# One copy of the folded weights per row group, token-major first sums, reciprocals on GpSimd, filler matmuls at the start

## The chip, the cores and the metric

The kernel runs on one core of one Trainium2 chip. The metric is the device time of one execution in microseconds (us), median of several runs. Engines are named as the profile names them: PE is TensorE (PEld its weight loads), ACT ScalarE, DVE VectorE, POOL GpSimd, SP SyncE, whose queue (SPq) issues 381 of the 400 DMA instructions in the trace of the kernel before. Each engine is given its own list of instructions.

## The reference, cut

Two stages of attention between 4 x 12416 tokens of 128 channels and 32 inducing points, then a gated feed-forward layer with 1536 hidden channels.

```python
def mab(q, kv):
    s = scale * (q @ kv.transpose(0, 2, 1))
    s = s - s.max(-1, keepdims=True)
    a = np.exp(s)
    a /= a.sum(-1, keepdims=True) + 1e-09
    return a @ kv
h = mab(I, x)                      # 32 rows per batch: sums over all tokens
attn = mab(x, h)                   # every token looks at the 32 rows
gate = 1.0 / (1.0 + np.exp(-(attn @ w_gate)))
return (gate * (attn @ w_val)) @ w_out
```

## The kernel before: the parts that matter

The second attention is never multiplied out. `h` is folded into the gate and value weights once per batch (`fold`), so a token needs only its 32 attention weights. The tokens are processed in units of 512 (25 units per batch, the last one a short tail of 128). A unit has six `G` steps (two gate matmuls, row-packed, into one of two PSUM buffers), six `T` steps (a 128x1024 tanh on ScalarE), twelve `V` steps (one value matmul into one of three PSUM buffers), twelve products (`D` on VectorE, or `C` on ScalarE with `P` on GpSimd), twelve `W` steps (four output matmuls each) and one evacuation of the accumulator `ACC` by ScalarE (`E`). Every engine's list is written out in a table `ORDER`, so the order was chosen ahead of time.

The fold, three times 1024 columns per batch, with `hT` (`h` transposed) repeated four times so that all four row groups of the array get both weights:

```python
hT = [sb(f"hT{q}", [P, 4, M]) for q in range(2)]
hw = [sb(f"hw{q}", [P, 2 * F]) for q in range(2)]
def fold(b, j, eng):
    def em(o):
        t = psl(o)
        for k, w in ((0, wg), (1, wv)):
            PE.matmul(t[:, k * TOK : (k + 1) * TOK], lhsT=hT[q][:].rearrange("c a m -> c (a m)"), rhs=w[:, j * TOK : (j + 1) * TOK],
                      start=True, stop=True)
    # ... one copy of 1024 columns to hw, on ACT (on DVE for j == 1 of batch 0)
```

The rows of a later quad (16 tiles of 128 tokens): score, exponential, a DMA transpose, a tree of sums on GpSimd, the reciprocal on VectorE, the multiplication on GpSimd, then more DMA:

```python
def tree(o):                                                     # on GpSimd
    # ... pairwise sums of 32 into TREE
    POOL.tensor_tensor(out=sm_b.t[:, 0:ng], in0=TREE[:, 0:ng, 0], in1=TREE[:, 0:ng, 1], op=ALU.add)
rc = dve(160, [tr] + rc_b.old, f"rc{b}.{i}", lambda o: DVE.reciprocal(out=rc_b.t[:, 0:ng], in_=sm_b.t[:, 0:ng]))
# ... mult(o) on GpSimd: n_b = t_b * rc_b, then bt (DMA transpose), wr, re (DMA)
```

Batch 0 does without DMA transposes in its first sums: x is transposed by TensorE, scores come out with the inducing points on the partitions, and TensorE transposes them back (`ap`) before the sums over tokens (`hp`). The three weights are cast by ScalarE (`wg`, `wv`, `wo`). Which products go to GpSimd: `COPIES = (3,)`, one of twelve in every unit. GpSimd's list begins with the casts of x and then, at once, the loads of batch 1 (`... cx5.8 cx5.0 ld1.0 ld1.1 tr0.1 mu0.1`).

The softmax here doesn't subtract the row's maximum and nothing guards it: scores larger than these inputs give would overflow.

## Time and profile before

| | |
|---|---|
| median of 3 runs | 714.0 us (712.83 to 714.18) |
| first tanh of the units | 31.65 us into the trace |
| eleventh evacuation of `ACC` | 122.3 us |
| end of the trace | 712.5 us |

The page of the kernel before: busy time of each engine with its share of the span, and the span in 40 slices of 17.8 us (a digit is the busy share in tenths; PEclk is the clock granted to TensorE).

```profile
PE 679.3 (95%) x7928; PEld 382.2 (54%) x7928; DVE 677.4 (95%) x1156; ACT 685.2 (96%) x884; POOL 336.5 (47%) x449
...
PE   5799999999999999999999999999999999999998
...
ACT  3989999999999999999999999999999999999994
POOL 6354446355354374364462642643634535526431
PEclk9959999999999999999999999999999999999999
```

Three engines are at 95%, and one slice near the start has half the clock. The view by windows of the kernel before (window, its length, busy us and instructions of each engine, granted clock, DMA share, GB/s):

```profile
0.00:31.65 31.65, 21.16 (x337) 14.69 (x338) 13.91 (x34) 18.81 (x30) 15.70 (x30) 1.00 0.95 318
31.65:34.50 2.85, 1.16 (x7) 0.28 (x5) 1.50 (x3) 2.85 (x5) 1.89 (x5) 1.00 0.25 49
34.50:51.60 17.10, 16.68 (x137) 7.63 (x136) 12.31 (x21) 14.49 (x18) 8.83 (x13) 0.50 0.60 96
51.60:122.30 70.70, 68.50 (x811) 37.89 (x808) 68.31 (x117) 70.56 (x95) 34.76 (x48) 1.00 0.79 148
122.30:702.00 579.70, 564.70 (x6555) 316.63 (x6552) 574.51 (x974) 576.99 (x739) 275.02 (x354) 1.00 0.40 96
```

The five busy figures are PE, PEld, DVE, ACT, POOL. From 34.5 to 51.6 us, at half clock, ScalarE is busy 14.49 of 17.10 us and VectorE 12.31. Afterwards both are nearly always busy. (At the very start the clock record has no entry yet; the first matmuls are slower all the same: a 512-wide score matmul takes 0.61 us at 12.4 us and 0.39 us at 18.1 us.)

The view of groups by form of the kernel before (count, then busy us in all, mean ns of one, and idle time before):

```profile
L625 DVE SCALAR_TENSOR_TENSOR ua<-tga,v 128x512 f16<-128x512 f16 x1056 | 648.7, 680 | 13.7 <-PE v L625 3.7 <-ACT tga L625 3.4 <-PE g L625 2.4
L625 ACT ACTIVATE tga<-g 128x1024 f16<-128x1024 f32 x576 | 562.0, 1078 | 3.5 <-PE v L625 1.0 <-PE g L625 0.5 <-ACT e L625 0.3
...
L625 ACT COPY vs<-v 128x512 f32<-128x512 f32 x96 | 60.9, 634 | 1.6 <-PE v L625 1.2
...
L625 ACT CAST hw<-g 128x1024 f16<-128x1024 f32 x11 | 11.6, 1059 | 0.1
...
L625 DVE RECIPROCAL rc<-sm 128x16 f32<-128x16 f32 x19 | 4.6, 244 | 0.0
```

A mean here is the span of one instruction, and neighbours overlap. The distance from start to start, where an engine has work queued, is what an instruction costs its engine: 0.904 us for the tanh, 0.466 for a 512-wide copy, 0.598 for a product on VectorE, 0.163 for a row reciprocal.

### The profile page before, as it was taken

To read this page: it belongs to the slowest core of one execution; us is meant where nothing else is said; L and a number is where in the kernel's file an instruction comes from. 1 tells how busy PE (TensorE), PEld (TensorE's weight loads), DVE (VectorE), ACT (ScalarE), POOL (GpSimd) and SP (SyncE) were. 2 spreads that over 40 slices of the span, in tenths; PEclk is the share of its full clock that TensorE was granted. 3 is DMA by queue.
4 is the path that set the end of the run, shared out by engine and by line. 5 is a ranking of instruction groups with operands and counts; after the bars stand their busy time and mean duration, and the time that the engine had idled before them with its cause. 6 is when DMAs were issued, how large, how long until landed. Compare 5 with 4: busy or idle time off the path is not lost.

```text
span 712.5 us, 20005 instructions
## 1 busy us (share of the span) xinstructions
PE 679.3 (95%) x7928; PEld 382.2 (54%) x7928; DVE 677.4 (95%) x1156; ACT 685.2 (96%) x884; POOL 336.5 (47%) x449
## 2 busy tenths in 40 slices
PE   5799999999999999999999999999999999999998
PEld 3445555555565555555555555555555555555555
DVE  2679999999999999999999999999999999999997
ACT  3989999999999999999999999999999999999994
POOL 6354446355354374364462642643634535526431
PEclk9959999999999999999999999999999999999999
DMA  9868769475445753456435464223221222131111
GB/s 360 213 111 149 129 133 187 113 133 102 111 115 99 168 112 70 117 131 132 106 97 102 94 148 98 69 85 96 62 74 62 85 68 90 46 122 59 52 61 50
DMA packets 113326, 78.63 MB, mean 110 GB/s; under 512 B 80560, under 2 KB 97360, under 8 KB 112592
## 3 DMA queue, kind: packets, MB, share of 16 engines
q1 hardware_dynamic: 110592, 67.80, 36.9%
q0 software_dynamic: 2592, 9.54, 8.6%
q8 instruction: 62, 1.02, 0.6%
q14 instruction: 32, 0.26, 0.1%
q10 hardware_dynamic: 48, 0.02, 0.0%
HBM read 39.99 MB, written 28.57 MB: 96 GB/s over the span
## 4 chain that ended last, share of the span: by engine, by line
PE 56%; DVE 27%; ACT 11%; issue 5%; DMA 1%; POOL 0%; ACTq 0%; SPq 0%; DVEq 0%
PE acc L625 27%; DVE ua L625 25%; PE v L625 20%; PE g L625 9%; ACT tga L625 8%; ACT os L625 2%; DMA xT<-in_x_dram 1%; ACT vs L625 1%; DVE ut L625 1%; ACT eT L625 0%; ACT hw L625 0%; ACT tgt L625 0%; ACT e L625 0%; DVE xT L625 0%; DVE hw L625 0%
## 5 line engine op out<-in xcount | busy, mean ns | idle before, releaser
L625 DVE SCALAR_TENSOR_TENSOR ua<-tga,v 128x512 f16<-128x512 f16 x1056 | 648.7, 680 | 13.7 <-PE v L625 3.7
L625 ACT ACTIVATE tga<-g 128x1024 f16<-128x1024 f32 x576 | 562.0, 1078 | 3.5 <-PE v L625 1.0
L625 PE MATMUL acc<-wo,ua 128*128 128x128 f16 x4608 | 362.4, 221 | 1.3
L625 PEld LDWEIGHTS <-ua 128*128 128x128 f16 x4608 | 262.6, 98 | 170.1 <-issue 160.9
L625 PE MATMUL v<-a2r,hw 32*128 32x512 f16 (+1 forms) x1200 | 327.6, 377 | 12.4 <-DVE ua L625 9.6
L625 POOL TENSOR_TENSOR pt<-tga,vs 128x512 f32<-128x512 f16 x96 | 111.7, 1164 | 296.8 <-ACT vs L625 208.6
L625 PE MATMUL g<-a2r,hw 32*128 32x512 f16 (+1 forms) x1200 | 227.0, 381 | 4.7 <-ACT tga L625 3.1
L625 PEld LDWEIGHTS <-hw 32*128 32x128 f16 x2400 | 89.7, 91 | 120.3 <-issue 55.7
L625 POOL TENSOR_TENSOR ua<-pt,vs 128x512 f16<-128x512 f32 x96 | 121.8, 1268 | 7.5
L625 ACT COPY os<-acc 128x512 f32<-128x512 f32 (+1 forms) x100 | 62.3, 623 | 6.8 <-PE acc L625 6.8
L625 ACT COPY vs<-v 128x512 f32<-128x512 f32 x96 | 60.9, 634 | 1.6 <-PE v L625 1.2
L625 POOL TENSOR_TENSOR a2n<-e2t,rc 128x128 f16<-128x128 f16 x96 | 37.2, 485 | 25.2 <-DVE rc L625 22.2
L625 POOL TENSOR_TENSOR tree<-tree 128x64 f32<-128x64 f32 (+4 forms) x69 | 23.8, 344 | 5.4
L625 POOL TENSOR_TENSOR tree<-e2t 128x256 f32<-128x256 f16 (+1 forms) x23 | 15.9, 690 | 20.2 <-DMA e2t<-e 20.2
L625 ACT ACTIVATE eT<-g 128x512 f16<-128x512 f32 (+1 forms) x26 | 15.7, 613 | 1.6 <-PE g L625 1.5
L625 PE MATMUL v<-ident,x 128*128 128x128 f16 x97 | 9.8, 270 | 7.4 <-POOL x L625 7.4
L625 ACT ACTIVATE e<-g 128x512 f16<-128x512 f32 (+1 forms) x23 | 15.8, 687 | 0.0
L625 DVE COPY xT<-v 128x1024 f16<-128x1024 f16 (+1 forms) x7 | 4.5, 651 | 11.7 <-PE v L625 11.6
L625 ACT COPY xT<-v 128x1024 f16<-128x1024 f16 (+1 forms) x6 | 5.8, 959 | 9.4 <-PE v L625 9.4
L625 PEld LDWEIGHTS <-x 128*128 128x128 f16 x114 | 8.4, 119 | 9.0 <-POOL x L625 8.5
L625 POOL DMA_DIRECT2D x<-in_x_dram x18 | 10.7, 596 | 3.0 <-PE v L625 2.9
L625 ACT CAST hw<-g 128x1024 f16<-128x1024 f32 x11 | 11.6, 1059 | 0.1
(77 smaller groups left out, 151.9 us busy)
## 6 DMA issues: line engine op xcount, KB each, us to landing
out_dram<-os SPq DMA_DIRECT2D x96, 256.0 KB, 2.4
a2r<-dr SPq DMA_DIRECT2D x92, 128.0 KB, 2.9
x<-in_x_dram POOLq DMA_DIRECT2D x15, 512.0 KB, 5.7
xT<-in_x_dram SPq DMA_DIRECT2D x3, 1024.0 KB, 9.1
dr<-a2p SPq DMA_DIRECT2D x19, 128.0 KB, 2.0
x<-in_x_dram POOLq DMA_DIRECT2D x3, 544.0 KB, 6.0
xT<-x SPq DMA_TRANSPOSE x75, 2.6
tga<-in_x_dram SPq DMA_DIRECT2D x1, 1024.0 KB, 5.1
```

The lines of the kernel that those rows point to most:

```text
L625: ins = fn(*a, **k)
```

## The change

The intent, part by part:

- Each row group of the array keeps only the weights that it uses, so a fold is one copy of 768 columns instead of three of 1024.
- Batch 0's scores come out token-major (`s1t`), so nothing has to be transposed back; sums over tokens come from a matmul against a column of ones. That column also replaces the accumulator reads in the later batches.
- The row reciprocals become a power of minus one on GpSimd, right after the tree.
- The weight casts go to GpSimd.
- Ten more products go to GpSimd: a second one in every eighth unit, none in the first two units (96 becomes 106).
- Ten groups of filler matmuls are put into TensorE's holes, meant to keep its clock up.
- All five lists of `ORDER` are new.

The diff, cut to its core:

```diff
-COPIES = (3,)
+def copied(b, u):
+    if b == 0 and u < 2:
+        return ()
+    return (3, 9) if u % 8 == 4 else (3,)
...  (ORDER: all lists new; GpSimd's now runs "... cx5.8 cx5.0 wg wv wo ld1.0 ld1.1 tr0.1 mu0.1 ...")
-    hw = [sb(f"hw{q}", [P, 2 * F]) for q in range(2)]
+    hw = [sb(f"hw{q}", [P, 6 * P]) for q in range(2)]
-    hT = [sb(f"hT{q}", [P, 4, M]) for q in range(2)]
+    hT = [sb(f"hT{q}", [P, M]) for q in range(2)]
...
+            for lo, n in ((0, 4), (4, 2)):
+                for r in range(4):
+                    w = (wg, wv)[r // 2][:].rearrange("c (j k f) -> c k j f", k=2, f=P)
+                    PE.matmul(t[32 * r : 32 * r + 32, lo * P : (lo + n) * P], lhsT=hT[q][:], rhs=w[:, r % 2, lo : lo + n, :],
+                              start=True, stop=True, tile_position=(0, 32 * r))
+        foldd[b] = [act(768, [m], f"fc{b}", lambda o: ACT.copy(out=hw[q][:], in_=psl(m)[:, 0:768]), give=m)]
...
+            POOL.tensor_tensor(out=sm_b.t[:, 0:ng], in0=sm_b.t[:, 0:ng], in1=minus1[:, 0:ng], op=ALU.pow)
-        rc = dve(160, [tr] + rc_b.old, f"rc{b}.{i}", lambda o: DVE.reciprocal(...))
...  (batch 0, per group of up to eight tiles: s1t, one exponential, then)
+                    for k in range(n):
+                        r = 32 * (k % 4)
+                        PE.matmul(ACC[r : r + 32, 0:P], lhsT=ae.t[:, k, :], rhs=buf.t[:, k0 + k, :], ...)
+                    for k in range(n):
+                        r = 32 * (k % 4)
+                        PE.matmul(ACC[r : r + 32, P : P + 1], lhsT=ae.t[:, k, :], rhs=ones16[:, 0:1], ...)
...
-        wl[nm] = act(F, [ld], nm, lambda o, n=n, dst=dst: ACT.copy(out=dst, in_=WS[n]))
+        wl[nm] = op("POOL", 1.5, [ld], nm, lambda o, n=n, dst=dst: POOL.tensor_copy(out=dst, in_=WS[n]))
...
+    def fill(o, n):
+        for _ in range(n):
+            PE.matmul(ACC[:, 384:512], lhsT=ident[:], rhs=ident[:], start=False, stop=False, skip_group_check=True)
```

## The prediction

> **What bounds the kernel now.** The page's busy shares are 95% (TensorE), 95% (VectorE), 96% (ScalarE). From 100 to 700 us the view by windows has ScalarE 99.5% and VectorE 99.1% busy, but busy spans of successive instructions overlap. Spacing from start to start, read from the trace, gives the true occupancy: a 128x1024 tanh 0.904 us, a 128x512 copy 0.466, a 512-wide VectorE multiply 0.598. At these spacings ScalarE needs 581 us of the 600 and VectorE 583: each waits only 3%. TensorE's row-packed matmuls wait for PSUM buffers, about 60 us of 600. So ScalarE and VectorE bind together. The first tanh starts at 31.65 us. The clock record is halved from 34.5 to 51.6 us; there ScalarE is busy only about 81% and VectorE 74% (windows of 2 us).
>
> **What the change does, costed.**
>
> 1. Start. Batch 0's scores go token-major, so transposes, their copies and the accumulator reads leave; the three weight casts (1.46 us each) leave ScalarE for an idle GpSimd. Two stood on the chain (at 22.4 and 26.2 us). Three folds of 1024 columns become one of 768, and two more row copies move to VectorE. hT should be ready near 24 us instead of 26.5, the first tanh near 28: −3.6 us.
>
> 2. Clock. Ten fillers (some 70 plain matmuls) fill TensorE's holes up to the first units. [...] its record changes at 17.5, 34.5 and 51.6 us, in steps of 17.07 us[...]. If the second drop vanishes, ScalarE regains about 19% of 17 us, 3.2 us. I give that 3 in 4: −2.4 us.
>
> 3. VectorE, main part. Copies to ScalarE and GpSimd go from 96 to 106: −10×0.598 = −6.0 us. 23 row reciprocals leave, at 0.165 us: −3.8. Sum reduces and narrower hT: −0.6. About −10 us (1.5%).
>
> 4. ScalarE, main part. Ten more copies: +4.7. Nine folds of 0.9 become three of about 0.68: −6.1. Accumulator reads leave (21, about 0.1 each): −2. One row copy: −0.5. About −4 us.
>
> 5. TensorE: folds −3, one-column sum matmuls +2; the count of changes between row-packed and full matmuls hardly moves (575 to 583 in the two orders). About zero. GpSimd: ten products at 2.43 us, and 23 powers: 47% to about 51%, harmless.
>
> **On the path.** ScalarE becomes the tighter of the two. With its present waiting the main part gains 4 us; with VectorE looser, its waiting should shrink too: I take −6. The tail's merged multiplies: −0.3. Sum: −3.6 −2.4 −6 −0.3 ≈ −12.3.
>
> **Prediction: 701.5 us, range 694 to 708.5.** Faster by over 2% (below 699.7): 0.40; within 2%: 0.58; slower by over 2%: 0.02.
>
> **What would show each step.** (1) First tanh between 27 and 29 us. (2) No halved clock after the first units begin; ScalarE above 92% busy from 34 to 52 us. (3, 4) VectorE's busy share falls below ScalarE's; from 100 to 600 us a unit (one evacuation of the output accumulator) takes about 1% less. (5) TensorE's idle time before value matmuls stays; GpSimd near 51%.
>
> **What would make it wrong.** Fillers that [...] sit in TensorE's queue ahead of the real chain; the power operation costing a microsecond or more; a new instruction order with worse or better interlocking: with three engines near 97%, the order matters as much as the sums. If TensorE's sequence sets the pace, the main part gains almost nothing (706); if ScalarE's waiting nearly vanishes, it gains over 12 us (695).

That fillers would keep the clock full, 3 in 4, was my estimate. What the trace of the kernel before shows is TensorE busy 1.16 of 2.85 us from 31.65 to 34.50 us and the clock halved right after it. Two more figures are estimates: the 0.68 us of a 768-column fold lies between the 0.466 us of a 512-wide copy and the 0.9 us of a 1024-wide one, and of the 60 us that TensorE's matmuls wait for PSUM buffers the list of waits names only 10.1 us (`V` for VectorE's products) and 3.3 us (`G` for the tanh).

## The result

| | before | after |
|---|---|---|
| median, 4 runs each | 714.09 us | 711.73 us |
| range | 712.83 to 714.4 | 710.61 to 713.06 |

The ratio after to before is 0.9971, with a 95% interval of 0.995 to 0.9992. (A ratio here is the mean time of one kernel's fast runs over that of the other's of the same rounds, so not quite the ratio of the medians that are quoted.) The change gains 2.4 us, a fifth of the 12.5 that were predicted.

The page of the kernel after, the same lines:

```profile
PE 674.6 (95%) x8413; PEld 388.1 (55%) x8413; DVE 666.5 (94%) x1121; ACT 673.8 (95%) x859; POOL 434.3 (61%) x495
...
PE   5898999999999999999999999999999999999997
...
ACT  3597999999999999999999999999999999999995
POOL 7374557575485584665774583765756756767351
PEclk9898999999999999999999999999999999999999
```

VectorE and ScalarE have 11 us less work each, as hoped, but GpSimd has 98 us more, 70 of them powers, and two of ScalarE's early slices are emptier (the second and the fourth: 5 and 7 where there were 9 and 9). The groups by form:

```profile
L631 DVE SCALAR_TENSOR_TENSOR ua<-tga,v 128x512 f16<-128x512 f16 x1046 | 643.2, 682 | 16.6 <-PE v L631 9.8 <-PE g L631 1.7 <-PE acc L631 1.1
L631 ACT ACTIVATE tga<-g 128x1024 f16<-128x1024 f32 x576 | 560.9, 1089 | 4.6 <-PE v L631 3.2 <-issue 0.5 <-PE g L631 0.2
...
L631 ACT COPY vs<-v 128x512 f32<-128x512 f32 x106 | 68.2, 643 | 0.0
...
L631 POOL TENSOR_TENSOR sm<-sm,minus 128x16 f32<-128x16 f32 x19 | 55.5, 2919 | 1.5
...
L631 ACT CAST hw<-g 128x768 f16<-128x768 f32 x4 | 3.2, 812 | 0.0
```

The fourth line is the power: 2.92 us for 16 elements per partition, where the addition of the same shape on the same engine takes 0.21 us. The windows of the kernel after:

```profile
0.00:33.08 33.08, 22.49 (x485) 19.71 (x489) 10.28 (x27) 13.46 (x26) 20.03 (x33) 0.90 0.83 287
34.50:51.60 17.10, 15.89 (x188) 8.49 (x186) 16.59 (x29) 17.05 (x20) 13.42 (x22) 1.00 0.38 56
57.00:67.30 10.30, 7.81 (x56) 3.70 (x55) 5.01 (x9) 5.66 (x8) 2.81 (x3) 0.67 0.98 150
67.30:125.00 57.70, 55.12 (x729) 30.96 (x724) 54.03 (x91) 56.30 (x72) 36.32 (x42) 1.00 0.75 149
125.00:702.00 577.00, 561.90 (x6815) 318.15 (x6815) 569.76 (x950) 573.74 (x726) 359.36 (x395) 1.00 0.41 97
```

The fillers did their work from 34.5 to 51.6 us: full clock, ScalarE busy 17.05 of 17.10. But there is a new hole at 57 to 67.3 us, where ScalarE is busy only 5.66 of 10.30, and the first tanh comes at 33.08 us, later than before.

To see where the time went, cut each trace (one profiled run of each kernel) at the first tanh and at the start of the eleventh evacuation:

| us | until first tanh | then to 11th evacuation | then to the end | trace |
|---|---|---|---|---|
| before | 31.65 | 90.6 | 590.3 | 712.5 |
| after | 33.08 | 92.0 | 585.1 | 710.2 |
| difference | +1.4 | +1.4 | −5.2 | −2.3 |
| predicted (my split) | −3.6 | about −3 | about −5.5 | about −12 |

The long third part did almost what was predicted. The miss of ten microseconds lies in the first 125 us, half of it before the first tanh. Three places in the trace stand out. The first, TensorE alone in the timeline of the kernel after (start, length, instruction, count, idle time before and what ended it):

```profile
17.51 0.28 PE L631 MATMUL acc<-x,ae 128*32 128x128 f16 x8
17.62 0.19 PE L631 MATMUL acc<-ones,ae 128*32 128x1 f16 x5
20.04 0.19 PE L631 MATMUL acc<-ones,ae 128*32 128x1 f16 x3 [2.23 <-issue]
20.16 1.04 PE L631 MATMUL g<-ident,x 128*128 128x128 f16 x8
```

TensorE stops in the middle of a run of eight matmuls that need nothing new, for 2.23 us, and the profile sees nothing that it waits for ("issue"). It is the 449th TensorE instruction in the record (weight loads and matmuls counted). The clock record is halved from 19.5 us, shortly before TensorE goes on, to 26.3 us. The second place:

```profile
57.47 0.39 PE L631 MATMUL g<-xT,indT 128*32 128x512 f16 x1
58.63 1.26 POOL L631 TENSOR_TENSOR ua<-pt,vs 128x512 f16<-128x512 f32 x1
58.85 2.58 SPq L631 DMA_TRANSPOSE xT<-x  x2
60.35 0.54 PE L631 MATMUL g<-xT,indT 128*32 128x512 f16 x3 [2.49 <-DMA xT<-x]
```

Here TensorE has reached the first score of batch 1, and three of its four matmuls wait 2.49 us for a DMA transpose of x. Everything behind them waits too, and then the clock is halved from 60.5 to 67.3 us. In the kernel before the same score ran at 54.5 us without a wait. Two transposes of x stood early in its DMA queue, in front of the first transpose of finished rows (`a2p`):

```profile
29.66 2.64 SPq L625 DMA_TRANSPOSE xT<-x  x2
54.48 0.40 PE L625 MATMUL g<-xT,indT 128*32 128x512 f16 x4
```

In the new list of the kernel after all of them stand behind `a2p`, which waits until GpSimd has finished the rows, the power included:

```profile
44.16 1.19 SPq L631 DMA_TRANSPOSE a2p<-a2n  x1
45.45 3.87 SPq L631 DMA_TRANSPOSE xT<-x  x3
```

GpSimd also issues the loads of batch 1 later, behind the weight casts (first the kernel before, then after):

```profile
23.23 1.37 POOL L625 DMA_DIRECT2D x<-in_x_dram  x2 [2.91 <-PE v L625]
27.64 1.30 POOL L631 DMA_DIRECT2D x<-in_x_dram  x2
```

The third place is smaller: one group of the new fillers stands in TensorE's list right behind the last sums that `hT` needs.

```profile
28.70 0.25 PE L631 MATMUL acc<-ae,x 128*128 128x32 f16 x4
28.80 0.72 PE L631 MATMUL acc<-ident 128*128 128x128 f16 x10
29.55 0.36 DVE L631 RECIPROCAL hden<-acc 128x32 f32<-128x32 f32 x1 [1.77 <-PE acc L631]
```

The reciprocal for `hT` starts 0.6 us after the last sum has ended (28.95 us), right when the tenth filler ends (29.51). The same holds in all eleven traces with that group (1.1 us where the clock is halved there); in the three without it (the kernel before, and e4_nofill and f3_bpow below) the reciprocal starts 0.04 to 0.05 us after the last sum.

The list of waits of the kernel after names the first two places, and two smaller waits:

```profile
PE g L631 <- DMA xT<-x: 2.5, 1, 2.5
PE acc L631 <- issue: 2.2, 1, 2.2
PE acc L631 <- ACT os L631: 1.7, 2, 1.0
PE acc L631 <- POOL ua L631: 1.3, 1, 1.3
```

### The profile page after: what moved, and what is told of

It reads as the page before. It is cut to its first block, busy times and chain, and to the rows that moved or that the text cites. A ratio compares the mean times of both kernels' runs of the same rounds, so it can differ in the third digit from the quotient of the medians.

```text
span 710.2 us, 20937 instructions
## 1 busy us (share of the span) xinstructions
PE 674.6 (95%) x8413; PEld 388.1 (55%) x8413; DVE 666.5 (94%) x1121; ACT 673.8 (95%) x859; POOL 434.3 (61%) x495
## 4 chain that ended last, share of the span: by engine, by line
PE 52%; DVE 22%; ACT 11%; issue 4%; POOL 3%; DMA 3%; SPq 1%; DVEq 0%; ACTq 0%; POOLq 0%
PE acc L631 27%; DVE ua L631 21%; PE v L631 18%; ACT tga L631 8%; PE g L631 7%; ACT os L631 2%; ACT vs L631 1%; DMA xT<-x 1%; SPq L631 1%; POOL sm L631 1%; DMA e2t<-e 1%; POOL ua L631 1%; DMA out_dram<-os 1%; POOL pt L631 1%; POOL tree L631 1%
## 5 line engine op out<-in xcount | busy, mean ns | idle before, releaser
L631 POOL TENSOR_TENSOR pt<-tga,vs 128x512 f32<-128x512 f16 x106 | 123.2, 1162 | 224.2 <-ACT vs L631 122.9
L631 POOL TENSOR_TENSOR ua<-pt,vs 128x512 f16<-128x512 f32 x106 | 134.4, 1268 | 9.9 <-PE acc L631 1.7
L631 POOL TENSOR_TENSOR sm<-sm,minus 128x16 f32<-128x16 f32 (+1 forms) x23 | 69.7, 3029 | 1.8
L631 ACT ACTIVATE os<-acc 128x512 f32<-128x512 f32 (+1 forms) x100 | 64.0, 640 | 6.9 <-PE acc L631 6.0
L631 ACT COPY vs<-v 128x512 f32<-128x512 f32 x106 | 68.2, 643 | 0.0
L631 POOL TENSOR_TENSOR a2n<-e2t,sm 128x128 f16<-128x128 f16 x96 | 37.2, 482 | 0.5
L631 PE MATMUL g<-ident,x 128*128 128x128 f16 x97 | 10.6, 280 | 7.0 <-POOL x L631 7.0
L631 DVE COPY xT<-g 128x1024 f16<-128x1024 f16 (+1 forms) x7 | 4.5, 650 | 12.2 <-PE g L631 12.2
L631 ACT COPY xT<-g 128x1024 f16<-128x1024 f16 (+1 forms) x6 | 5.8, 960 | 9.6 <-PE g L631 9.6
```

Source lines behind the costliest of these rows:

```text
L631: ins = fn(*a, **k)
```

## The experiments

Two chips were used besides the first. The kernel before gave 714.0 to 714.9 us in the median beside each set, with single fast runs of up to 723 us at a lower clock. That makes the intervals 0.5 to 0.85% to each side; the three parts of the trace, which come from one profiled run of each kernel, are read beside them.

### The power and the two stops

Four kernels, run together, three rounds.

**e1_rc**: the reciprocals back on VectorE.

```diff
-            POOL.tensor_tensor(out=sm_b.t[:, 0:ng], in0=sm_b.t[:, 0:ng], in1=minus1[:, 0:ng], op=ALU.pow)
+        rc = dve(160, [tr] + rc_b.old, f"rc{b}.{i}", lambda o: DVE.reciprocal(out=rc_b.t[:, 0:ng], in_=sm_b.t[:, 0:ng]))
   (and 23 entries rc put into VectorE's list)
```

> The changed kernel with the row reciprocals back on VectorE (23 of about 0.17 us) in place of the power on GpSimd, which the trace shows at 3.03 us each (70 us in all). Theory A (the 3 us power makes GpSimd's row chain late: it holds the transposes queued behind it at the start, so the first score of batch 1 waits 2.5 us at 57.9 us and the clock halves after it, and it makes two later waits of 1.0 and 1.3 us for GpSimd's products): the waits at 58, 84 and 149 us go, GpSimd falls from 61% to about 52%, the time falls by 4 to 7 us to 705 to 708. Rival B (those stalls come from the order of the DMA queue and of TensorE, not from the power; VectorE pays 4 us more): the 58 us wait stays, time within 2 us of 711.7. The stall at 17.8 us stays under both.

Measured: 712.85 us, ratio to before 0.9956 (0.99 to 1.0013). GpSimd fell to 51%. The GpSimd wait at 149 us is gone, so that part of theory A holds. The wait for the transposes at 58 us is gone too, but this run does not show that the power caused it: TensorE reached the score only at 61.30 us, after its stop at the 449th instruction had lasted 3.5 us and the clock had been halved again from 50.5 us. The last two transposes that the score needs were issued at 50.09 us, as in the kernel after (50.05), and landed at 57.25 us instead of 60.31. The time did not fall. A wait of 2.1 us for another transpose appeared at 82 us, the middle part took 93.5 us against 92.0, and from the eleventh evacuation to the end it took 584.5 us against 585.1. Taking the power out, at the price of 23 reciprocals on VectorE, is worth nothing measurable in the long part of *this* kernel.

**e2_pow2**: each power run twice, the second into a scratch tile.

```diff
+            POOL.tensor_tensor(out=PW2[:, 0:ng], in0=sm_b.t[:, 0:ng], in1=minus1[:, 0:ng], op=ALU.pow)
             POOL.tensor_tensor(out=sm_b.t[:, 0:ng], in0=sm_b.t[:, 0:ng], in1=minus1[:, 0:ng], op=ALU.pow)
```

> The changed kernel with each power run twice (the second into a scratch tile that nobody reads). GpSimd gets 70 us more, to about 70%. Theory A: the row chain is 3 us later again, the waits at the start and the later waits for GpSimd's products grow, +4 us or more, 716 or above. Rival B (GpSimd's lateness is hidden): within 2 us of 711.7.

Measured: 769.33 us, ratio 1.0732. GpSimd's 70 us more cost 57 us. TensorE's waits for GpSimd's products rise from 1.3 us to 25.4, as the list of waits of this run shows, and a halved stretch of the clock record begins close to eight of the twelve:

```profile
PE acc L632 <- POOL ua L632: 25.4, 12, 4.8
```

So GpSimd was not idle at 61% in any useful sense: the first 3 us per quad fit in front of its deadlines, the second 3 us do not.

**e3_few** and **e4_nofill**: without the first four groups of fillers, and without any.

```diff
-  ... zero fill4.0 xt0.8 fill12.1 xt1.8 s1t0.8 fill5.2 xt1.0 s1t0.0 s1t1.8 fill3.3 hv0.0 ...
+  ... zero xt0.8 xt1.8 s1t0.8 xt1.0 s1t0.0 s1t1.8 hv0.0 ...     (e4_nofill: the other six as well)
```

> The changed kernel without the first four groups of fillers (24 matmuls, 48 TensorE instructions, all before 14 us). Theory C (the 2.2 us gap on TensorE at 17.6 to 20.0 us, in mid-run of unsynchronised matmuls at about the 449th recorded instruction, is TensorE's instruction stream running dry): the gap stays at about the 449th recorded instruction, so it moves to later work (48 instructions further in the program), and gets shorter or stays. Rival D (the gap is a wait for data or a semaphore at that place of the program): it stays in front of the same matmul, some 48 recorded instructions earlier, about 401. Time: 709 to 713.

> The changed kernel without any filler. If the fillers keep the clock up once the units begin: the clock record is halved for 7 to 17 us somewhere between 30 and 52 us, and the time is 2 to 4 us longer (714 to 716). If they do nothing: the same clock record after 30 us and a time within 1 us of 711.7.

Measured for e3_few: 714.19 us, ratio 1.0 (0.9916 to 1.0084). The stop stays at recorded instruction 449, which is now a different piece of work, again in mid-run. TensorE in the timeline of this run:

```profile
16.98 0.44 PE L642 MATMUL g<-ident,x 128*128 128x128 f16 x5
18.47 0.33 PE L642 MATMUL g<-ident,x 128*128 128x128 f16 x3 [1.05 <-issue]
```

There is a second one at instruction 705, that is 256 further, and the same two places, 449 and 705, show in e4_nofill. A wait for data would stay with its matmul; this one stays with the count. So rival D is out, and what fits is theory C: TensorE's instruction stream runs dry. The DMA records agree: packets of 16,384 bytes of the kind "instruction" land in the region, one of them at 18.57 us in the kernel after, 1.5 us before TensorE goes on. There are nine such stops in six runs, and in each TensorE goes on 1.3 to 1.5 us after such a packet has landed. In the kernel before, which does not stop, it lands at 21.31 us, and the 449th instruction is due at about 23.6. The pages count 62 of these packets (queue q8) in the kernel before and 66 in the kernel after, for 15,856 and 16,826 recorded TensorE instructions: one to 256 and one to 255, which agrees with the distance of the two stops. The stop of the kernel after falls into the time in which x and the weights fill the DMA queues (a DMA share of 0.98 to 1.09 from 14 to 20 us). That the loads are what makes the packet late was not tested by itself.

Measured for e4_nofill: 718.54 us, ratio 1.0036 (0.9963 to 1.0108), 4 us above e3_few in the median, with overlapping ranges (714.29 to 723.19 against 712.22 to 720.53). In the profiled run, its slowest, the clock was halved from 25.0 to 48.9 us and the middle part took 96.7 us. With the fillers the clock was full from 34.5 to 51.6 us (the kernel after; f5_bfill too), without them its mean was 0.58 from 31.92 to 52 us; what they are worth in time is measured better in f5_bfill below.

### Each mend alone, and two parts of the change alone

**f1_sums**: e3_few, and batch 0's sums by two wide matmuls for eight tiles instead of eight of one column (120 instructions fewer).

```diff
-                    for k in range(n):
-                        r = 32 * (k % 4)
-                        PE.matmul(ACC[r : r + 32, P : P + 1], lhsT=ae.t[:, k, :], rhs=ones16[:, 0:1], ...)
+                    for k in range(0, n, 4):
+                        PE.matmul(ACC[:, P : 2 * P], lhsT=ones16[:], rhs=ae.t[:, k : k + 4, :].rearrange("p s m -> p (s m)"), ...)
-        sbc = ... tensor_scalar_mul(out=ssb[0][:], in0=ones[:], scalar1=hacc[0][:, P : P + 1])
+        sbc = ... tensor_reduce(out=sred[:], in_=ACC[:, P : 2 * P].rearrange("p (k m) -> p m k", m=M), axis=AX.X, op=ALU.add)
-            PE.matmul(hsum, lhsT=ssb[0][:], rhs=I4[:], ...)
+            PE.matmul(hsum, lhsT=odiv[:], rhs=sred[:], ...)      # odiv is 1/128 throughout
```

> The changed kernel without the first four groups of fillers and with batch 0's sums made by two 128-column matmuls against a matrix of ones for eight row tiles, in place of eight one-column matmuls: 120 + 48 TensorE instructions fewer before the first units. Theory C (instruction fetch sets TensorE's pace while the loads fill the DMA queues[...]): the gaps at recorded instructions 449 and 705 shrink from 2.2 us together to under 1 us, the first tanh comes at 29.5 to 31.5 us instead of 33.1, time 707 to 710. Rival (the prologue is bound by the loads and the casts, and the gaps only hide waiting that would come anyhow): first tanh within 0.7 us of the 32.2 us of the kernel with fewer fillers, time unchanged.

Measured: no stop at 449 or 705, and the first tanh at 29.92 us, 3.2 us earlier than in the kernel after (the 168 instructions that were taken out count in this too). And yet 714.22 us, ratio 0.9987 (0.9927 to 1.0047), no gain. The list of waits says where the 3.2 us went:

```profile
PE g L644 <- DMA xT<-x: 5.0, 1, 5.0
```

The score of batch 1 waits until 59.7 us, much as in the kernel after (60.35 us); TensorE merely arrives there earlier. The wait was 2.5 us and is now 5.0, the clock is halved from 57.2 to 67.4 us, 10.2 us instead of 6.8, and once more for 3.4 us from 87.9 us. The middle part takes 98.5 us instead of 92.0. Here the gain in front of a fixed deadline turned into waiting.

**f2_sp**: the kernel after with the loads of batch 1 taken from behind the weight casts in GpSimd's list, and its first transposes moved up in the DMA queue.

```diff
  POOL: -... cx5.0 wg wv wo ld1.0 ld1.1 tr0.1 ...
        +... cx5.0 wg ld1.0 ld1.1 wv wo tr0.1 ...
  SP:   -... et0.1 et0.2 bt0.1 xd1.0.2 xd1.0.3 xd1.0.0 wr0.1 xd1.1.0 xd1.0.1 ...
        +... et0.1 xd1.0.0 xd1.0.1 xd1.0.2 xd1.0.3 xd1.1.0 et0.2 bt0.1 wr0.1 ...
  (and in load_quad these loads depend on the cast of wg instead of that of wo)
```

> The changed kernel with only the order of its loads and transposes altered: batch 1's first two loads issue right after the first weight cast instead of after the third, and the first five transposes of x stand ahead of the second row transpose in the DMA queue. The power stays. If the wait of 2.5 us at 57.9 us is one of queue order and late loads: it is gone, the clock stays full there, and the time falls by 3 to 5 us to 707 to 709. If it is owed to the 3 us power alone: most of the wait stays, time within 2 us of 711.7.

Measured: 709.57 us in the median of the three fast runs (one of four was slow, 716.99), ratio 0.9905 (0.9841 to 0.9969). The wait at 58 us is gone: the transposes are issued from 33.77 us and have landed by 42.3, and the middle part takes 87.8 us instead of 92.0, with the power still in place. The first tanh, however, came at 34.78 us, 1.7 us later still: the instruction stream stopped twice, 2.3 us (before the new loads were issued) and 0.7 us (after), and the clock was halved a second time from 28.3 to 35.1 us.

**f3_bpow**: the kernel before with the power in place of its reciprocals, and nothing else.

```diff
+            POOL.tensor_tensor(out=sm_b.t[:, 0:ng], in0=sm_b.t[:, 0:ng], in1=minus1[:, 0:ng], op=ALU.pow)
-        rc = dve(160, [tr] + rc_b.old, ...)          (and the 23 rc out of VectorE's list)
```

> The kernel before, with the power on GpSimd in place of the reciprocals on VectorE, and nothing else. Step 3 of the prediction counted this part as 3.8 us won on VectorE and harmless on GpSimd: about 711. Theory A (3.03 us in GpSimd's row chain, 70 us in all, delays rows and products): no gain or a loss, 713 to 722, with TensorE waits for GpSimd's results over 0.5 us that the kernel before does not have.

Measured: 733.36 us, ratio 1.0248 (1.0181 to 1.0314). One cheap-looking line costs the kernel before 19 us, nearly all in the third part (608.2 us against 590.3), and the waits for GpSimd's products appear that it did not have. The clock record is also halved for 24 us in all after 125 us, where the kernel before has under 1 us:

```profile
PE acc L638 <- POOL ua L638: 7.5, 7, 2.2
```

Set beside e1_rc this is the sharpest pair: in the order of instructions of the kernel before the power costs 19 us, in that of the kernel after nothing that could be measured. A likely reason, not tested by itself: the new `ORDER` gives GpSimd's products more time before their `W` steps are due. In TensorE's list 41.5 steps on average lie between the `V` step of such a product and its `W` step, against 36.3 before.

**f4_bfill** and **f5_bfill**: the kernel before with fillers only. In f4_bfill the last group was put behind the first `W` step, so it added to the first unit's sums; the result was wrong (relative error 53). f5_bfill leaves that group out and is correct. It was run later, five rounds.

```diff
-  ... sb0.1 fo0.1 s2t1 s2t0 fo0.2 fo0.0 rp0 rp1 G0.0.2 V0.0.4 G0.0.0 V0.0.1 V0.0.0 G0.0.4 G0.1.2 G0.0.1 ...
+  ... fill10.0 sb0.1 fo0.1 s2t1 s2t0 fill6.1 fo0.2 fo0.0 fill9.2 rp0 fill4.3 rp1 G0.0.2 V0.0.4 G0.0.0 V0.0.1 V0.0.0 fill7.4 G0.0.4 fill7.5 G0.1.2 fill7.6 G0.0.1 ...
```

> The kernel before with 55 filler matmuls in TensorE's holes from 25.5 to 35 us, and nothing else: step 2 of the prediction alone. Expected: the clock record does not halve from 34.5 to 51.6 us, ScalarE's busy share there rises from 81% to above 92%, and the time falls by 2.5 to 4 us. [...] halved as before, time within 1 us of the kernel before.

(The last outcome, "halved as before", was for the case that the fillers do nothing for the clock.)

> The kernel before with 50 fillers only, the run with fillers mended: the last group, which fell into the first unit's sums and spoilt them, is left out. Correct results. Expected as there: no long halved stretch after 30 us, 1.5 to 3 us faster than the kernel before, less than the 3.2 us worked out because the fillers delay the first tanh by about a microsecond.

Measured: f4_bfill 712.03 us, f5_bfill 711.93 us with ratio 0.9936 (0.9883 to 0.9988). The halved stretch shrinks to 27.1 to 30.5 us. The window that was at half clock, now in the run of f5_bfill:

```profile
34.50:51.60 17.10, 15.94 (x180) 8.51 (x180) 15.35 (x26) 17.10 (x22) 7.41 (x10) 1.00 0.72 87
```

ScalarE is busy all of it. The middle part takes 87.3 us against 90.6, a gain of 3.4; the first tanh comes 1.4 us later, at 33.04 us, and the third part is unchanged. Step 2's size was right, but in the place where these fillers stand they give back 1.4 us of it.

### The mends together

**h1_both** is f1_sums with f2_sp's moves. **h2_sums_sp** has only the moves in the DMA queue, with the loads left behind the weight casts. **h3_all_rc** is h1_both with the reciprocals on VectorE. Their edits are those shown above; five rounds.

> The two mends together: fewer TensorE instructions in the prologue (wide sums, no early fillers) and batch 1's loads and transposes moved ahead. If the two losses are separate terms, they add: first tanh near 30 to 31 us (33.1 in the changed kernel), no wait over 1 us near 58 us, time 702 to 706, that is about the predicted 701.5. If a third limit stands behind them in the first 60 us: 707 to 710.

> As h1_both, but the loads of batch 1 stay behind the weight casts; only the transposes are moved in the DMA queue. If the queue order is what delayed the score of batch 1: within 2 us of h1_both. If the late loads did: a wait of over 1 us for the transposes stays near 55 us, and the time is 2 to 5 us above h1_both.

> h1_both with the row reciprocals on VectorE again in place of the power. With the start mended, this isolates the power: if it costs what it cost the kernel before (19 us), this is well below h1_both, under 698; if the changed kernel's instruction order hides it, as the run with VectorE reciprocals suggested, within 2 us of h1_both, for VectorE's 3.8 us against GpSimd's waits.

| | median us | ratio to before | first tanh | to 11th evacuation | to the end |
|---|---|---|---|---|---|
| h1_both | 706.99 | 0.9865 (0.9813 to 0.9918) | 29.18 | 90.2 | 586.1 |
| h2_sums_sp | 712.2 | 0.9944 (0.9884 to 1.0004) | 29.71 | 92.5 | 585.4 |
| h3_all_rc | 705.77 | 0.9853 (0.98 to 0.9906) | 29.14 | 88.8 | 584.6 |

Moving the transposes without the loads is not enough: h2_sums_sp stays 5.2 us above h1_both in the median, with ranges that do not overlap (708.97 to 714.33 against 704.62 to 708.18; its profiled run was one of its fastest, 709.35 us). So the late loads cost time: GpSimd issues them at 22.98 us in h1_both and at 28.05 us in h2_sums_sp, behind the casts. But not by the wait that was expected: in h2_sums_sp the score of batch 1 runs at 56.88 us without a wait, so it was the order of the DMA queue, not the loads, that made it wait in the kernel after. What its trace does show is a clock halved from 45.9 to 52.8 and from 80.1 to 86.9 us; how the late loads lead there stays open. In h1_both the score runs at 53.56 us without a wait. Its time, 707.0, is at the edge of the two outcomes (702 to 706 if the losses add up, 707 to 710 if a third limit stands behind them), so some of the loss, about 2 us in the middle part by the side of f2_sp, is not accounted for (the only halved stretch there lasts 3.4 us, from 87.0 us). h3_all_rc is the fastest kernel and beats both; against h1_both it gains 1.2 us in the median, with overlapping ranges (704.39 to 707.51 against 704.62 to 708.18), so the power is close to free in this order.

## Why the prediction was wrong, point by point

**What bounds the kernel: right, as far as the runs show.** ScalarE and VectorE bind the long part together. The third part fell by 5.2 us in the kernel after and by 4.2 to 5.8 us in the seven of its descendants whose clock stays full there until the last few us, whatever happened at the start; the prediction had 6 us for the whole main part. The separate shares of folds, copies and reciprocals in it were not measured, and no run separates the smaller work from the new `ORDER`, so the agreement of the sum may be partly luck.

**Step 1, "hT should be ready near 24 us instead of 26.5, the first tanh near 28: −3.6 us": wrong, and the largest miss.** hT was ready at 30.14 us. Two things were missed. First, token-major sums need more TensorE instructions, and 449 recorded instructions were used up at 17.6 us instead of about 23.6 in the kernel before, while the instruction packet landed only at 18.57 us. The stop of 2.2 us, the halved clock after it and the extra instructions together cost 3.2 us of the first tanh (f1_sums). Second, even without the stop hT was ready only at 26.2 us (h1_both), as in the kernel before at 26.5: the prediction added up the work that was taken away, not the work that put its end where it was. The last copies of the transposed x begin at 21.6 us in h1_both and at 21.45 in the kernel before; no run moved them, so that they set the end of `hT` is argued. From there to `hT` the new chain takes 4.6 us instead of 5.1, and about 0.55 us of those 4.6 are the fillers in front of the reciprocal: the prediction's own warning of fillers that "sit in TensorE's queue ahead of the real chain" came true. What did get shorter is the stretch from hT to the first tanh, from 5.1 to 2.9 us, by the casts and folds that left ScalarE; that part of the step was right.

**Step 2, the clock, −2.4 us (3.2 times three quarters): right in effect and size, but not kept.** By themselves the fillers took the granted clock from 0.50 to 1.00 between 34.5 and 51.6 us, worth 3.4 us in the middle part (f5_bfill). In the kernel after it was lost again between 57 and 67.3 us. I also misread the clock record: its changes lie 17.07 us apart in the kernel before, but that is no step of its own: it is five times 3.413 us, and in the kernel after the stretches are 6.827 and 34.133 us, twice and ten times that.

**Steps 3 and 5, "GpSimd: ... 23 powers: 47% to about 51%, harmless": wrong.** A power takes 3.03 us in the mean, GpSimd went to 61%. I had costed it like the addition beside it. "The power operation costing a microsecond or more" stood among the prediction's risks, not in its sum. In the kernel before it would have cost 19 us (f3_bpow); the new order hides almost all of that, which nobody had planned and so was luck, but it had no room for a second (e2_pow2). At the start one power stands in front of the transposes that the first score waited for (39.57 to 42.50 us in the kernel after); what that cost is not shown, since e1_rc was disturbed by its longer stop.

**Not foreseen at all: a transfer with a date.** The new list of the DMA queue put every transpose of batch 1's x behind the first transpose of finished rows, which waits for GpSimd and its power: the first was issued at 45.45 us instead of 29.66. So the first score waited 2.5 us and the clock fell for 6.8 us. Of 10.3 us ScalarE lost 4.6. With the transposes moved ahead the wait is gone, with early loads (f2_sp) and with late ones (h2_sums_sp). Step 1 also moved the weight casts to "an idle GpSimd". GpSimd had idle time (it was busy for 47% of the span), but its list also issues the loads of batch 1, and they were put behind the casts: 27.64 us instead of 23.23. With the queue mended that costs 5.2 us (h2_sums_sp against h1_both). The prediction looked at that engine's load and not at what it triggers.

The sum, then: +1.4 instead of −3.6 before the first tanh, +1.4 instead of about −3 up to the eleventh evacuation, −5.2 instead of about −5.5 after it. With both stops mended the kernel reaches 705.8 to 707.0 us, inside the range that was predicted for the change itself (694 to 708.5); that is another kernel, and no support for the prediction as it stood.

What stays open: whether the loads are the reason that the instruction packet came late, how the late loads of batch 1 cost time once the transposes are moved, and the 2 us or so that h1_both still loses in its middle part.

## What to carry to other kernels

An engine with idle time may still be the one that starts a transfer (here GpSimd, whose loads of batch 1 came 4.4 us later): before giving it work, look at what stands behind that work in its list, and in the queues that wait for it, and when that is due. A saving counts only up to the next thing with a fixed date, so ask of each one which wait will absorb it; here 3.2 us at the start became 2.5 us of waiting 25 us later and a slower clock. Before counting on an operation that the trace does not show on that engine, measure it: one power on GpSimd was 14 times the addition of its shape.

## What the runs show of the power, the instruction stream and the clock

- A power on GpSimd took 2.92 us for 128x16 and 3.55 us for 128x20 in fp32, against 0.21 us for an addition of 128x16, and 0.24 us for VectorE's reciprocal of 128x16.
- While loads filled the DMA queues (a DMA share of 0.98 to 1.09 from 14 to 20 us in the kernel after), TensorE stopped at recorded instruction 449 and again, in some runs, at 705: nine stops in six runs, of 0.7 us (f2_sp) to 3.5 us (e1_rc), with about 71 instructions per us used just before the stop in the kernel after (14 to 17.8 us).
- The stretches in the clock record are whole multiples of 3.413 us (the halved ones 1, 2, 3, 5 and 7 times, but for the last piece of each record). Halved stretches of 6.83 us each came with the stops of 2.23 and 2.49 us in the kernel after, and in h2_sums_sp the record halves at 45.9 us after 3.4 us in which TensorE was busy 3.08 us. The one of the kernel before lasted 17.07 us, after a stretch with TensorE busy 1.16 of 2.85 us and although it was busy 16.68 of 17.10 us in it; what sets these lengths no run shows.
